# First loads, early spectrum, inverse tables and first norms of a two-layer conv and FFN kernel rearranged

## The chip, the cores and the metric

The kernel runs on one core of one Trainium2 chip. Its time is device microseconds per execution, the median over the runs. A profiled execution gives a span (first to last instruction) and a trace of every engine: PE (TensorE), DVE (VectorE), ACT (ScalarE), POOL (GpSimd) and SP (which only issues DMAs).

## The reference

Two layers, each a gated long convolution (A) and a SwiGLU block (B), on 2048 rows of 512 channels in bf16:

```python
def _A_ref(q, k, v, shift_k, ssm_k, ssm_D):
    # k_shift: a causal shift filter of 4 taps per channel
    for t in range(ks):
        k_shift = k_shift + k_pad[:, t:t + S, :] * shift_k[:, ks - 1 - t][None, None, :]
    kv = k_shift * v
    ...  # y = causal convolution of kv with ssm_k over 2048 rows, by FFTs of 4096
    y = y + kv * ssm_D[None, None, :]
    return q * y

def _B_ref(x, w_gate, w_up, w_down):
    return (_silu(x @ w_gate) * (x @ w_up)) @ w_down      # 512 -> 1792 -> 512

x = A_q
x = x + _A_ref(_layernorm(x), A_k, A_v, A_shift_k, A_ssm_k, A_ssm_D)
x = x + _B_ref(_layernorm(x), B_w_gate, B_w_up, B_w_down)
x = x + _A_ref(_layernorm(x), A_k, A_v, A_shift_k, A_ssm_k, A_ssm_D)
x = x + _B_ref(_layernorm(x), B_w_gate, B_w_up, B_w_down)
```

The convolution y does not depend on x, so it is computed once and serves both layers.

## The kernel before, in words

**Blocks.** The 2048 rows are cut into NB = 4 blocks of 512 rows. A block lies on the 128 partitions with R = 4 consecutive rows on each (row = 4p + r), 512 channels along the free dimension. The convolution is done block by block with transforms of length 1024 written as matmuls: `fwd` holds 14 tables of 128x128 (cosine and sine for each residue r, and their negatives), `inv` the same tables transposed. For each block the kernel makes the spectrum of its filter block h (`H`, `G`), the spectrum of its k-shifted times v rows (`X`), the products of spectra that meet in an output block (`Z`), and the inverse (`Y`).

**Start of the program, block 0.** What runs first needs the first loads and tables that are made on the chip.

- The loads: `load_k(0)` (L361) and `load_h(0)` (L356) and the row of ssm_D (`drow`) on ACT's DMA queue, in this order; the taps (`tapR`), `load_v(0)` and `load_x(0)` on SP's. The gate weights `wg` go to SP's queue too, but a one-element copy on POOL (L901) that reads h and writes `wg_sb` holds them until h has landed. Behind them on SP's queue: h and k of block 1, `wu`, `wd`.
- The tables: POOL makes index ramps, DVE the phases `ph` (8 blocks, L908, L913), ACT takes the Sin (two halves of `fwd`, L915), DVE the negated blocks (L921). `inv` comes from 14 PE transposes of `fwd` (L957) and two ACT copies (L959).
- The shift filter as matmuls: the taps are turned on PE (`turn_taps`), and for each 128 channels (`dt`) and each tap j a diagonal matrix `dg[dt, j]` is made from the identity: 3 groups on DVE (L937), the fourth on ACT (L934, four activations). k is turned with 16 PE transposes (`transpose_k`, L379) and copied to `kTb`. `shift_mul` (L487) is then 64 matmuls of 128 columns into four PSUM tiles, each multiplied into `vt` on DVE (L503).
- h is turned with 16 PE transposes (`transpose_h`, L476), copied to `hs`, and `drow` is added to its row 0 (L943). `half` (L430) makes half of h's spectrum with 8 matmuls of 512 columns; twice, with `butterfly` behind each on DVE. `direct` (L454) makes X in 32 matmuls, `product` Z on DVE (L621, L625), `inverse_direct` (L684) Y in 32 matmuls with `inv`.
- The layer norms of block 0's rows: `ln_stats` on DVE (bn_stats L707), the power of -0.5 on POOL (L712), `normalise` on DVE (L755). There is a form on ACT as well, `ln_stats_act` (L716), with accumulating activations.

**FFN units.** Each (layer, block, half block of 256 rows) is a unit `ffn` (L808): 112 matmuls of 256 columns for gate and up, Silu and copies on ACT, a product on DVE (L845), and 28 matmuls of 512 columns with `wd`, added to x by DVE (L871), or, for units in X_PE, by two more matmuls with the identity (L818). 16 units follow each other; the convolution work of the next blocks is put between their instructions.

**Order.** All instructions are first entered in a plan (`add`) with an engine, an assumed cost, an assumed latency for DMAs (`lat`), an optional due time, and PSUM or SBUF rings that they need. `forward` then plays the plan through and picks, engine by engine, the order of issue; the chip's engines run their instructions in this order. Constants steer it: DUR and T0 (due times of the units), STRETCH, HSL, ASL, SLK, and the sets ST1, ST2, Z_ACT, N_ACT, X_PE that say which engine does a norm or an addition. While the plan has PE idle before 32 us, `issue` fills the gap with matmuls of the identity (`wm`, L1024):

```python
n = int((start - t - 0.4) / 0.085)
```

Of the kernel before, what the change touches and what calls it, by code (L numbers as in the profile page):

```python
# [9 lines left out]
P = 128  # L10
# [9 lines left out]
SLK = 9.39  # L20
H_DMA = lambda b: b in {2, 3}
ST1 = lambda l, c, h: (l, c, h) in {(0, 2, 0), (0, 3, 1), (1, 0, 1)}
ST2 = lambda l, c, h: (l, c, h) in {(0, 1, 0), (0, 1, 1), (0, 3, 1), (1, 0, 0)}
ASL = 4.93
# [4 lines left out]
HSL = 8.56  # L29
Z_ACT = lambda l, c, h: (l, c, h) in {(0, 1, 1), (0, 3, 0), (0, 3, 1), (1, 0, 0), (1, 0, 1), (1, 1, 1), (1, 2, 0), (1, 2, 1), (1, 3, 1)}  # L30
N_ACT = lambda l, c, h: (l, c, h) in {(0, 2, 1), (0, 3, 0), (0, 3, 1), (1, 1, 0), (1, 3, 0)}
Z_DMA = lambda i, j: False
D_DMA = lambda l, c, h: False
X_PE = lambda l, c, h: (l, c, h) in {(0, 2, 0), (0, 2, 1), (1, 3, 1)}
RINGS = {}
T0, FLOOR = -4.91, -25.25
DUR = [25.78, 17.38, 27.0, 25.33, 24.61, 20.95, 21.66, 16.0, 20.19, 21.8, 21.11, 25.85, 19.67, 26.45, 17.91, 25.24]
STRETCH = {1: {"PE": 5.28, "DVE": 1.49, "ACT": 3.3, "POOL": 1.0, "SP": 110.68},
           2: {"PE": 1.3, "DVE": 1.9, "ACT": 1.37, "POOL": 1.0, "SP": 1.4},
           3: {"PE": 2.03, "DVE": 1.56, "ACT": 1.6, "POOL": 1.0, "SP": 1.97}}  # L40
R = 4
# [3 lines left out]
NS = 8  # L45
# [21 lines left out]
class Plan:  # L67
# [182 lines left out]
    def issue(self, seq, place, when, warm_until, warm):  # L250
        t, busy = 0.0, {}
        for o in seq:
            start, end = when[o]
            if o.eng == "PE":
                if start < warm_until and start - t > 0.5:
                    for ring, i in [(r, i) for r in ("pf", "pd", "pc") for i in range(self.rings[r])]:
                        if busy.get((ring, i), 0.0) <= t:
                            n = int((start - t - 0.4) / 0.085)
                            if n > 0:
                                warm(ring, i, n)  # L260
                            break
                t = end
# [9 lines left out]
def kernel(  # L272
# [70 lines left out]
    tapT, drow = whole("tapT", [P, KD, KS]), new("jk", "drow", [1, D])  # L343
# [12 lines left out]
    def load_h(b, eng="SP", due=None, after=()):  # L356
        hn[b] = new("s8" if b == 1 else "h", "hn", [P, KD, L], parts=1)
        q = nc.sync if eng == "SP" else nc.scalar
        return add(eng, 0.55, lambda: q.dma_start(out=hn[b].t[:], in_=h3[:, :, b * L:(b + 1) * L]), w=[hn[b]], lat=(5.5, 10.0)[b] if b < 2 else 6.0, due=due, after=after)

    def load_k(b, due=None, after=()):  # L361
        if b == 0:
            kn[b] = new("s8", "kn", [P, R, D])
            add("ACT", 0.5, lambda: nc.scalar.dma_start(out=kn[b].t[:], in_=k_t[:, b]), w=[kn[b]], lat=4.6, due=due)
            return
# [4 lines left out]
    def transpose_k(b, ring, engs):  # L370
# [3 lines left out]
        for dt in range(KD):  # L374
            pt = new(ring, "pt", [P, R, P], BF16)
# [13 lines left out]
    def load_v(b, due=None, after=()):  # L389
        vt[b] = new("v", "vt", [P, R, D], parts=R)  # L390
        return add("SP", 0.6, lambda: nc.sync.dma_start(out=vt[b].t[:], in_=v_t[:, b]), w=[vt[b]], lat=4.5 if b else 5.0, due=due, after=after)

    def load_x(c, due=None, after=()):
        xs[c] = new("x", "xc", [P, R, D], parts=R)
        return add("SP", 0.7, lambda: nc.sync.dma_start(out=xs[c].t[:], in_=q_t[:, c]), w=[xs[c]], lat=4.5 if c else 6.0, due=due, after=after)
# [34 lines left out]
    def half(rows, ev, par, scale, ring, engs, conv):  # L430
        for ch in ("ac", "bd")[par]:
            slot = "abcd".index(ch)
            for part in (0, 1):
# [3 lines left out]
                    r=[(rows, [r for _, r in terms]), fwd], w=[ps], conv=conv)  # L437
# [16 lines left out]
    def direct(rows, dst, ring, engs):  # L454
        for slot in (0, 2, 1, 3):
            c1, c2, sign = (("a", "c", 1), ("b", "d", 1), ("a", "c", -1), ("b", "d", -1))[slot]
            for part in (0, 1):
# [3 lines left out]
                add("PE", pe(4), lambda ps=ps, terms=terms: mm(ps.t[:], [(fT(f, r), rows.t[:, r, :]) for f, r in terms]),  # L461
                    r=[rows, fwd], w=[ps])
# [3 lines left out]
    def transpose_h(b, ring, order, conv, engs=("ACT",)):  # L466
        hs = new("hs", "hs", [P, R, D], parts=R)
        m = len(engs)
        for r0 in order:
# [9 lines left out]
            if engs[order.index(r0) % m] == "ACT":  # L479
                add("ACT", act(len(rows) * D), lambda pt=pt, sl=sl: nc.scalar.copy(out=hs.t[:, sl, :], in_=pt.t[:]),  # L480
                    r=[pt], w=[(hs, rows)], conv=conv)
            else:
# [4 lines left out]
    def shift_mul(b, ring, conv, after=()):  # L487
        for r in range(R):
# [7 lines left out]
            add("PE", pe(KS * KD, P), go, r=[kT[b], dg], w=[ps], conv=conv, after=after)  # L496
            if KV_ACT and b:
# [3 lines left out]
                    [ks], [(vt[b], (r,))], conv=conv)  # L501
                continue
            dve(D, lambda ps=ps, r=r: nc.vector.tensor_tensor(out=vt[b].t[:, r, :], in0=ps.t[:], in1=vt[b].t[:, r, :],  # L503
                                                             op=ALU.mult), [ps], [(vt[b], (r,))], one=True, conv=conv)
# [90 lines left out]
    def spectrum_x(b):  # L595
        if K_ACT(b):
            shift_mul_t(b)
        else:
            shift_mul(b, "pc", True, first if b == 1 else ())
# [84 lines left out]
    def inverse_direct(k, slots_order):  # L684

        y, z = new_y(k), Z[k]
        pss = [new(("pd", "pd", "pc", "pc")[r], "ps", [P, D], F32) for r in range(R)]
# [28 lines left out]
    def ln_stats_act(c, rows):  # L716
# [3 lines left out]
        for o, i in enumerate(rows):  # L720
            jk = new("jk", "jk", [P, D])
            add("ACT", 0.62, lambda jk=jk, o=o, i=i: nc.scalar.activation(
                out=jk.t[:], in_=xs[c].t[:, i, :], func=ACT.Copy, accum_out=sm.t[:, o:o + 1]), r=[(xs[c], (i,))], w=[jk, (sm, (o,))])
# [17 lines left out]
    def shift_of(st, n):  # L741
# [3 lines left out]
                                                                op0=ALU.mult, op1=ALU.mult), r=[mv, rstd], w=[nmr])  # L745
# [15 lines left out]
    def apply_norm(c, h, layer=0):  # L761
        rows = range(HP * h, HP * h + HP)
        st = ln_stats_act(c, rows) if ST1(layer, c, h) else ln_stats(c, rows)
        nmr = shift_of(st, HP) if N_ACT(layer, c, h) else None
# [5 lines left out]
    def prologue(layer, c, h, on_pe=False):  # L770
# [21 lines left out]
        st = ln_stats(c, rows)  # L792
        done = []
        for o, i in enumerate(rows):
# [7 lines left out]
            pop = add("PE", pe(KD, P), go, r=[z, ident], w=[pt])  # L802
            add("ACT", act(D), lambda pt=pt, o=o: nc.scalar.copy(out=zT.t[:, :, o, :], in_=pt.t[:]), r=[pt], w=[(zT, (o,))])
            done = [zop, pop]
        return done


    def ffn(unit):  # L808
# [81 lines left out]
    load_k(0, -70)  # L890
    tapR = new("dn", "tapR", [KD, P, KS])
    add("SP", 0.5, lambda: nc.sync.dma_start(out=tapR.t[:], in_=A_shift_k.rearrange("(dt p) j -> dt p j", p=P)), w=[tapR],
        lat=4.3, due=-70)
    load_h(0, "ACT", -59)
    ph = new("s8", "ph", [P, NS, P], I32, parts=2)
    load_v(0, -59)
    add("ACT", 0.5, lambda: nc.scalar.dma_start(out=drow.t[:], in_=A_ssm_D.rearrange("(o d) -> o d", o=1)), w=[drow], lat=5.0,
        due=-58)
    load_x(0, -58)

# [157 lines left out]
```

## Time and profile before

| | |
|---|---|
| median of 5 runs | 354.87 us (354.57 to 355.17) |
| profiled execution | 355.17 us, span 353.4 us |
| PE busy | 347.8 us (98%), 2716 matmuls |
| DVE busy | 276.5 us (78%) |
| ACT busy | 249.7 us (71%) |
| POOL busy | 38.5 us (11%), 42 instructions |
| HBM read, written | 12.33 MB, 2.10 MB |

Busy times of PE are modelled (matmuls are pipelined), so the spacing of starts tells more than the share. In the chain of waits each step is what released the next one; "issue" is time in which an engine waited for nothing that the profile shows. In a table by stage, each engine's busy time stands with its number of instructions in brackets.

### The profile page before, as it was taken

Reading aid. Unit: us, or ns where it says so; the run is one execution under the profiler, and the core shown is the slowest. Engines: PE = TensorE matmul, PEld = TensorE weight load, DVE = VectorE, ACT = ScalarE, POOL = GpSimd, SP = SyncE. Lnnn points to the kernel's source line nnn. Section 1 sums busy time; section 2 is a strip of 40 time slices with the busy share of each in tenths; the row PEclk is TensorE's granted clock in tenths of the full one; section 3 lists DMA queues with packets and bytes.
Section 4 is the critical chain, followed back from the end, with each engine's and each line's share of the span. In section 5 each row is a group of like instructions: output and inputs, shape, how many; then the busy total and the mean of one; then the engine's idle time right before and its main releaser. Section 6 shows DMA issues by size and latency. Waiting matters only on the chain.

```text
span 353.4 us, 6784 instructions
## 1 busy us (share of the span) xinstructions
PE 347.8 (98%) x2716; PEld 255.0 (72%) x2716; DVE 276.5 (78%) x511; ACT 249.7 (71%) x470; POOL 38.5 (11%) x42
## 2 busy tenths in 40 slices
PE   7999999999999999999999999999999999999996
PEld 7745976867778686858677676758687777778673
DVE  4997999999989999999997999799973323545111
ACT  4768684859897865758869994946488975646452
POOL 1001010111102110111220010201111000001000
PEclk9999999999999999999999999999999999999999
DMA  6999230010333222012101033010102010101100
GB/s 238 294 346 302 48 81 10 2 30 2 72 109 77 76 89 32 0 32 60 32 32 31 14 108 61 0 32 1 32 30 32 30 32 1 24 8 24 38 2 30
DMA packets 37898, 21.98 MB, mean 62 GB/s; under 512 B 29798, under 2 KB 35691, under 8 KB 37867
## 3 DMA queue, kind: packets, MB, share of 16 engines
q1 hardware_dynamic: 37192, 20.51, 22.2%
q10 hardware_dynamic: 674, 1.05, 0.9%
q8 instruction: 21, 0.34, 0.4%
q14 instruction: 11, 0.08, 0.1%
HBM read 12.33 MB, written 2.10 MB: 41 GB/s over the span
## 4 chain that ended last, share of the span: by engine, by line
PE 65%; DVE 26%; ACT 4%; issue 2%; POOL 2%; ACTq 0%; DVEq 0%; POOLq 0%
PE pf L335 36%; PE pd L852 18%; PE ps L335 8%; DVE ht L845 3%; DVE bnst L707 3%; DVE m L519 2%; DVE t L636 2%; DVE t L652 2%; DVE t L642 2%; ACT H L424 2%; DVE Z L657 2%; PE wm L1024 2%; DVE G L556 1%; DVE xc L778 1%; POOL rstd L712 1%
## 5 line engine op out<-in xcount | busy, mean ns | idle before, releaser
L335 PE MATMUL pf<-zT,wg_sb 128*128 128x256 bf16 x896 | 116.1, 273 | 0.2 <-ACT sg L838 0.2
L335 PE MATMUL pf<-zT,wu_sb 128*128 128x256 bf16 x896 | 116.1, 273 | 0.0
L852 PE MATMUL pd<-wd_sb,ht 128*128 128x512 bf16 x448 | 103.1, 379 | 0.0
L335 PEld LDWEIGHTS <-wg_sb 128*128 128x128 bf16 x896 | 87.6, 98 | 19.3 <-issue 0.7
L335 PEld LDWEIGHTS <-wu_sb 128*128 128x128 bf16 x896 | 87.6, 98 | 11.4
L838 ACT ACTIVATE sg<-pf 128x512 bf16<-128x512 f32 x112 | 67.6, 604 | 26.0 <-PE pf L335 25.8
L842 ACT CAST ht<-pf 128x512 bf16<-128x512 f32 x112 | 66.2, 591 | 18.6 <-PE pf L335 18.1
L852 PEld LDWEIGHTS <-ht 128*128 128x128 bf16 x448 | 43.8, 98 | 47.1
L845 DVE TENSOR_TENSOR ht<-ht,sg 128x1024 bf16<-128x1024 bf16 x64 | 39.4, 619 | 33.3 <-ACT ht L842 33.3
L712 POOL TENSOR_TENSOR rstd<-ve,nhalf 128x2 f32<-128x2 f32 x25 | 29.1, 1163 | 207.0 <-DVE ve L710 185.8
L707 DVE BATCH_NORM_STATS2 bnst<-xc 128x6 f32<-128x512 bf16 x50 | 32.3, 684 | 0.5
L864 ACT CAST dn<-pd 128x512 bf16<-128x512 f32 x26 | 14.0, 590 | 25.0 <-PE pd L852 25.0
L636 DVE TENSOR_TENSOR t<-X,G 128x2048 bf16<-128x2048 bf16 x18 | 21.9, 1218 | 0.0
L642 DVE TENSOR_TENSOR t<-X,G 128x2048 bf16<-128x2048 bf16 x18 | 21.9, 1218 | 0.0
L871 DVE TENSOR_TENSOR xc<-xc,dn 128x1024 bf16<-128x1024 bf16 x13 | 8.9, 688 | 15.9 <-ACT dn L864 15.8
L424 ACT ACTIVATE X<-ps 128x512 bf16<-128x512 f32 x32 | 18.6, 604 | 2.0 <-PE ps L335 1.9
L751 ACT ACTIVATE z<-xc,nmr,rstd 128x512 bf16<-128x512 bf16 x18 | 13.6, 807 | 2.8 <-DVE nmr L744 2.7
L737 POOL TENSOR_TENSOR rstd<-ve,nhalf 128x2 f32<-128x2 f32 x7 | 7.8, 1118 | 70.4 <-DVE ve L733 70.4
L335 PE MATMUL ps<-vt,fwd 128*128 128x512 bf16 x56 | 15.2, 379 | 0.0
L335 PEld LDWEIGHTS <-fwd 128*128 128x128 bf16 x96 | 9.3, 98 | 7.9 <-issue 0.2
L652 DVE TENSOR_TENSOR t<-t,t 128x2048 bf16<-128x2048 bf16 x12 | 14.7, 1222 | 0.1
L657 DVE TENSOR_TENSOR Z<-Z,t 128x2048 bf16<-128x2048 bf16 x12 | 14.7, 1221 | 0.1
(96 smaller groups left out, 318.0 us busy)
## 6 DMA issues: line engine op xcount, KB each, us to landing
vt<-in_A_v_dram SPq DMA_DIRECT2D x4, 512.0 KB, 4.0
xc<-in_A_q_dram SPq DMA_DIRECT2D x4, 512.0 KB, 4.8
out_dram<-xc SPq DMA_DIRECT2D x16, 128.0 KB, 1.8
wg_sb<-in_B_w_gate_dram SPq DMA_DIRECT2D x1, 1792.0 KB, 7.5
wu_sb<-in_B_w_up_dram SPq DMA_DIRECT2D x1, 1792.0 KB
wd_sb<-in_B_w_down_dram SPq DMA_DIRECT2D x1, 1792.0 KB, 13.5
hn<-in_A_ssm_k_dram SPq DMA_DIRECT2D x3, 512.0 KB, 6.1
kn<-in_A_k_dram ACTq DMA_DIRECT2D x1, 512.0 KB, 3.3
```

Source lines behind the costliest of these rows:

```text
L335: nc.tensor.matmul(o, lhsT=lhsT, rhs=rhs, start=(n == 0), stop=(n == len(terms) - 1))
L424: add("ACT", act(D), lambda: nc.scalar.activation(out=view(), in_=ps.t[:], func=ACT.Copy, scale=scale), r=[ps], w=[(buf, keys)], conv=conv)
L636: dve(n * D, lambda t1=t1, part=part: nc.vector.tensor_mul(out=t1.t[:], in0=x.t[:, sl, 0, :], in1=g.t[:, sl, part, :]), [(x, key(slots, (0 ...
L642: dve(n * D, lambda t2=t2, part=part: nc.vector.tensor_mul(out=t2.t[:], in0=x.t[:, sl, 1, :], in1=g.t[:, sl, 1 - part, :]), [(x, key(slots ...
L652: dve(n * D, lambda t1=t1, t2=t2, comb=comb: nc.vector.tensor_tensor(out=t1.t[:], in0=t1.t[:], in1=t2.t[:], op=comb), [t2], [t1], conv=conv)
L657: dve(n * D, lambda t1=t1, part=part: nc.vector.tensor_add(out=z.t[:, sl, part, :], in0=z.t[:, sl, part, :], in1=t1.t[:]), [t1], [zk], con ...
L707: add("DVE", 0.6, lambda st=st, i=i: nc.vector.bn_stats(out=st.t[:], in_=xs[c].t[:, i, :]), r=[(xs[c], (i,))], w=[st])
L712: add("POOL", PW, lambda: nc.gpsimd.tensor_tensor(out=rstd.t[:], in0=ve.t[:], in1=nhalf.t[:].to_broadcast((P, n)), op=ALU.pow), r=[ve, nha ...
L838: add("ACT", act(D), lambda ps=ps, o=o, sg=sg: nc.scalar.activation(out=sg.t[:, o:o + 2, :], in_=ps.t[:], func=ACT.Silu), r=[ps], w=[(sg, ...
L842: add("ACT", act(D), lambda ps=ps, o=o, ht=ht: nc.scalar.copy(out=ht.t[:, o:o + 2, :], in_=ps.t[:]), r=[ps], w=[(ht, (o // 2,))], due=(uni ...
L845: dve(n * W, lambda sg=sg, ht=ht: nc.vector.tensor_mul(out=ht.t[:], in0=ht.t[:], in1=sg.t[:]), [sg], [ht], due=(unit, k / pairs, 0.0, "h"))
L852: nc.tensor.matmul(pds[o].t[:], lhsT=ht.t[:, q, o * P:(o + 1) * P], rhs=wt["d"].t[:, ft, :], start=(ft == 0 and not xpe), stop=(ft == NF - 1))
```

## The change

- h of block 0 is the first and, but for `drow`, the only load on ACT's queue; k goes to SP's queue, behind the taps and ahead of v and x. The copy on POOL that held `wg` is gone; `wg` follows x on SP's queue.
- `inv` comes from two DMA transposes of `fwd` on SP's queue, behind `wg` and ahead of h and k of block 1, `wu` and `wd`; the 14 PE transposes and two ACT copies go.
- h is turned first, its row 0 is copied together with the addition of `drow` (now 128 rows of zeros but for the first), and half "ac" of its spectrum is entered ahead of the taps and of k. The other half, "bd", comes behind the shift and the first slot of `direct`. The `direct` matmuls are entered in groups of two terms.
- The diagonals of two `dt` go to POOL (8 instructions), two stay on DVE; the two negations of table blocks go to POOL.
- The norms of block 0 in layer 0, both halves, are taken on ACT, the second half after the first half's z.
- The filler's count, several assumed latencies and due times, PSUM rings, the constants and the engine sets are new.

```diff
-SLK = 9.39
+SLK = 8.59
-ST1 = lambda l, c, h: (l, c, h) in {(0, 2, 0), (0, 3, 1), (1, 0, 1)}
-ST2 = lambda l, c, h: (l, c, h) in {(0, 1, 0), (0, 1, 1), (0, 3, 1), (1, 0, 0)}
-ASL = 4.93
+ST1 = lambda l, c, h: (l, c, h) in {(0, 2, 0), (0, 3, 0), (1, 0, 1)}
+ST2 = lambda l, c, h: (l, c, h) in {(0, 1, 0), (0, 1, 1), (1, 0, 0)}
+ASL = 2.32
-HSL = 8.56
-Z_ACT = lambda l, c, h: (l, c, h) in {(0, 1, 1), (0, 3, 0), (0, 3, 1), (1, 0, 0), (1, 0, 1), (1, 1, 1), (1, 2, 0), (1, 2, 1), (1, 3, 1)}
-N_ACT = lambda l, c, h: (l, c, h) in {(0, 2, 1), (0, 3, 0), (0, 3, 1), (1, 1, 0), (1, 3, 0)}
+HSL = 18.8
+Z_ACT = lambda l, c, h: (l, c, h) in {(0, 1, 1), (0, 3, 0), (0, 3, 1), (1, 0, 0), (1, 0, 1), (1, 1, 1), (1, 2, 0), (1, 2, 1)}
+N_ACT = lambda l, c, h: (l, c, h) in {(0, 3, 0), (0, 3, 1), (1, 1, 0), (1, 3, 0), (1, 3, 1)}
-X_PE = lambda l, c, h: (l, c, h) in {(0, 2, 0), (0, 2, 1), (1, 3, 1)}
+X_PE = lambda l, c, h: (l, c, h) in {(0, 1, 0), (0, 1, 1), (0, 2, 1), (1, 3, 1)}
...
-                            n = int((start - t - 0.4) / 0.085)
+                            n = int((start - max(t, 1.0) - 0.3) / 0.106)
...
-        return add(eng, 0.55, ..., w=[hn[b]], lat=(5.5, 10.0)[b] if b < 2 else 6.0, due=due, after=after)
+        return add(eng, 0.55, ..., w=[hn[b]], lat=(4.1, 10.0)[b] if b < 2 else 6.0, due=due, after=after)
...
-            add("ACT", 0.5, lambda: nc.scalar.dma_start(out=kn[b].t[:], in_=k_t[:, b]), w=[kn[b]], lat=4.6, due=due)
+            add("SP", 0.5, lambda: nc.sync.dma_start(out=kn[b].t[:], in_=k_t[:, b]), w=[kn[b]], lat=4.2, due=due)
...
-            pt = new(ring, "pt", [P, R, P], BF16)
+            pt = new("pc" if dt < 2 else "pd", "pt", [P, R, P], BF16)
...
-        pss = [new(("pd", "pd", "pc", "pc")[r], "ps", [P, D], F32) for r in range(R)]
+        pss = [new(("pd", "pd", "pf", "pf")[r], "ps", [P, D], F32) for r in range(R)]
...
-    load_k(0, -70)
+    load_h(0, "ACT", -70)
     tapR = new("dn", "tapR", [KD, P, KS])
...
-        lat=4.3, due=-70)
-    load_h(0, "ACT", -59)
+        lat=3.4, due=-70)
+    load_k(0, -69)
...
     load_v(0, -59)
+    add("POOL", 0.3, lambda: nc.gpsimd.memset(drow.t[:], 0.0), w=[drow], due=-60)
...
-    load_x(0, -58)
-    add("POOL", 0.1, lambda: nc.gpsimd.tensor_copy(out=wt["g"].t[0:1, 0, 0:1], in_=hn[0].t[0:1, 0, 0:1]), r=[hn[0]], w=[wt["g"]])
-    wg = load_weights("g", -57)
+    x0 = load_x(0, -58)
...
-        add("DVE", 0.28, lambda src=src, dst=dst: nc.vector.tensor_scalar(
+        add("POOL", 0.6, lambda src=src, dst=dst: nc.gpsimd.tensor_scalar(
             out=fwd.t[:, dst, :], in0=fwd.t[:, src, :], scalar1=-1.0, scalar2=None, op0=ALU.mult),
             r=[(fwd, (n,))], w=[(fwd, (part,))])
+    wg = load_weights("g", -57, after=[x0])
+    for n in range(2):
+        sl = slice(n * NI, (n + 1) * NI)
+        tabs = add("SP", 2.2, lambda sl=sl: nc.sync.dma_start_transpose(
+            out=inv.t[:, sl, :], in_=fwd.t[:, sl, :].rearrange("p k f -> p (k f)")), r=[fwd], w=[(inv, (n,))], lat=8.0, due=-56.8,
+            after=[wg])
+    load_h(1, "SP", -56.5, after=[tabs])
+    load_k(1, -56.4, after=[tabs])
+    load_weights("u", -56, after=[tabs])
+    load_weights("d", -55, after=[tabs])
+    hs = transpose_h(0, "pf", (0, 2, 1, 3), False, ("DVE", "ACT"), drow)
+    ev = spectrum("ev")
+    G[0] = H[0] = spectrum("G0")
+    half(hs, ev, "ac", 2.0 / N, "pf", ("ACT", "DVE"), False, -60)
...
-    for j in range(KS):
-        add("ACT", 0.32, lambda j=j: nc.scalar.activation(out=dg.t[:, KD - 1, j, :], in_=ident.t[:], func=ACT.Copy,
-                                                          scale=tapF.t[:, KD - 1, j:j + 1]), r=[ident, tapF], w=[(dg, (KD - 1,))])
-    for dt in range(KD - 1):
+    for dt in (KD - 2, KD - 1):
+        for j in range(KS):
+            add("POOL", 0.35, lambda dt=dt, j=j: nc.gpsimd.tensor_scalar(out=dg.t[:, dt, j, :], in0=ident.t[:],
+                                                                         scalar1=tapF.t[:, dt, j:j + 1], scalar2=None, op0=ALU.mult),
+                r=[ident, tapF], w=[(dg, (dt,))])
+    for dt in range(KD - 2):
...
+    transpose_k(0, "pc", ("ACT", "DVE"))
+    shifted = shift_mul(0, "pf", False, due=-49)
+    normed[0, 0, 0] = apply_norm(0, 0, on_act=True, due=-47)
+    butterfly(ev, G[0], 0, False)
     X[0] = spectrum("X0")
-    direct(vt[0], X[0], "pf", ("ACT", "ACT"))
+    direct(vt[0], X[0], "pf", ("ACT", "ACT"), (0,))
+    half(hs, ev, "bd", 2.0 / N, "pf", ("ACT", "ACT"), False)
+    butterfly(ev, G[0], 1, False)
+    direct(vt[0], X[0], "pf", ("ACT", "ACT"), (2, 1, 3))
...
-    first = prologue(0, 0, 0, True)
+    first, stats = prologue(0, 0, 0, True)
+    normed[0, 0, 1] = apply_norm(0, 1, on_act=True, after=first)
     prologue(0, 0, 1)
```

DUR, STRETCH, T0 (-4.91 to -8.68) and FLOOR are new as well.

## The prediction

> **What bounds the kernel now.** I read the page's 40 slices first, then the PE timeline, the chain of waits, the windows, and the DMA issues of the first 9 us. PE is busy in every slice:
>
> ```profile
> PE   7999999999999999999999999999999999999996
> PEclk9999999999999999999999999999999999999999
> ```
>
> The PE timeline shows what it does (start, us, instructions):
>
> ```profile
> 1.73 5.35 PE L1024 MATMUL wm<-ident 128*128 128x128 bf16 x51 [1.73 <-POOL ident masks.py:199]
> 7.33 1.07 PE L379 MATMUL pt<-ident,kn 128*128 128x128 bf16 x16
> ...
> 9.24 1.11 PE L476 MATMUL pt<-ident,hn 128*128 128x128 bf16 x12
> ...
> 10.53 3.73 PE L335 MATMUL ps<-dg,kTb 128*128 128x128 bf16 x64
> 14.10 3.73 PE L335 MATMUL ps<-hs,fwd 128*128 128x512 bf16 x16
> ...
> 35.89 1.03 PE L335 MATMUL pf<-zT,wg_sb 128*128 128x256 bf16 x8
> ```
>
> From 10.53 the matmuls start back to back. Spacings in the timeline are 0.109 us (256 columns), 0.216 (512) and 0.058 (128). From 35.89 to 350.0 there are 1792 of 256, 518 of 512 and 112 shift matmuls of 128 columns: 195.6 + 111.9 + 6.5 = 314.0 us in a stretch of 314.1. From 10.53 to 35.89 the same count gives 25.0 of 25.4. So retuned constants (DUR, HSL, the sets) have no idle PE time to recover after 10.53; they can only lose some. What can be gained lies ahead of 10.53, and there the chain of waits reads:
>
> ```profile
> 1.73 5.37 PE wm L1024 x51
> ...
> 7.79 0.46 issue
> 8.24 0.98 ACT dg L934 x3
> 9.23 0.47 ACT kTb L384
> 9.70 0.30 ACT dg L934
> 10.00 0.48 ACT hs L480
> ...
> 10.53 14.20 PE ps L335 x112
> ```
>
> PE runs 51 filler matmuls (wm) until 7.08; its queue is in order, so the k transposes wait for them. But k had landed long before:
>
> ```profile
> vt<-in_A_v_dram SPq DMA_DIRECT2D x1, 512.0 KB, 4.2
> xc<-in_A_q_dram SPq DMA_DIRECT2D x1, 512.0 KB, 6.4
> ...
> kn<-in_A_k_dram ACTq DMA_DIRECT2D x1, 512.0 KB, 3.3
> hn<-in_A_ssm_k_dram ACTq DMA_DIRECT2D x1, 512.0 KB, 6.8
> ```
>
> With the issue starts added (0.73, 1.16, 1.17, 1.59) k lands at 4.0, v at 5.4, h at 8.0, x at 8.0. The filler's end, some 3 us after k, is what starts the kernel, and h at 8.0 is next.
>
> **The start, step by step.** I compare the moment T at which the 64 shift matmuls start: 10.53 now, and from there PE is full. In the changed kernel the first half of the h spectrum (8 matmuls x 0.216 = 1.73) is done before T, so the end moves by 10.53 + 1.73 - T = 12.26 - T.
>
> *Filler.* The count is int((4.8 - 0.4)/0.085) = 51 now (tapR planned at 0.5 + 4.3). With 3.4 for tapR, and max(t, 1.0) in it, it becomes int((3.9 - 1.0 - 0.3)/0.106) = 24; with a few more before h, PE is released at about 4.5 to 5.0.
>
> *h.* It was second on ACT's queue and landed at 8.0; first there, k would have been its row: 4.0. It now shares the engines with tapR and k on SP's queue. The windows show 53 GB/s in 1 to 2 us, 315 in 2 to 3, some 400 after; equal shares of 1.05 MB end near 4.7. Its 1 KB rows against k's 4 KB make it later rather than earlier. I take 4.9, between ends 4.1 and 8.0. k then takes v's place (5.4), v about 6.6, x stays near 8.0, as the total bytes are the same.
>
> *PE before T.* 4 tap transposes (0.25), 16 of h, 16 of k, 8 matmuls of 512. At full rate: 0.25 + 0.91 + 0.91 + 1.73 = 3.8. But the filler runs at 5.35/51 = 0.105 us each, and the k transposes after 7.33 at 0.057: the PE is at half rate until about 7, though the PEclk row shows 9 throughout. What is done before 7 therefore costs double. From 4.9, 16 of h end at 6.6 and 3 of k by 6.9; 13 x 0.057 more end at 7.6, the spectrum half at 9.4, with the taps 9.6. The hs copies (0.6 each, two engines, from 5.5) are ready by 7.2, under the k transposes.
>
> The Trainium skill, "TensorE: Matmul & The Clock Gate", Part 1, says the clock opens after about 3.4 us of sustained activity, in a free-running window. That speaks against starting real work early; with a start at 1.73 it would put the opening anywhere in 5.1 to 8.5, and T between 8.8 and 10.4 by an estimate from that page.
>
> *GpSimd.* It gets the two negations (128x384), the drow memset and 8 tap diagonals. No such row exists in the trace; the nearest are
>
> ```profile
> 1.38 0.29 POOL masks.py:199 TENSOR_SCALAR_AFFINE_SELECT ident<-ident 128x128 bf16<-128x128 bf16 x1
> 15.90 0.70 POOL L712 TENSOR_TENSOR rstd<-ve,nhalf 128x2 f32<-128x2 f32 x1 [7.37 <-DVE ve L710]
> ```
>
> and the groups' mean of 1.163 us for rstd beside a busy DVE. The first has the right shape: I take 0.35 to 0.5. Negations from 4.3 (the first Sin ends there) to 5.7, then 8 x 0.35 to 0.5 ends at 8.5 to 9.7: just under PE's 9.6. "SBUF — State Buffer", Who interferes with whom, has DVE and GpSimd exclude each other on a shared port where DVE reads two SBUF inputs. By that page only the two DVE diagonals (0.64 each) and the row-0 add's like would block, an estimated 1.3 us more, T near 10.5.
>
> *DVE before T.* Two hs (0.66 + 0.64), taps 0.2, two dg 1.28, two kTb 1.28: 4.1 us from 5.5 is 9.6 at the latest. Three engines meet at 9.6, so T = 9.7 and the gain is 2.56 us.
>
> **The rest.** The 14 table transposes leave PE, but they stood in the hole before 10.53; PE gains nothing, ACT 1.74 us that it was not short of. X_PE grows from three to four units: 2 x 0.216 = 0.43 us more on PE in the full stretch. Sum: 2.56 - 0.43 = 2.13.
>
> The inverse tables go to SP's queue. SP waits there for the negations (to 5.7) and behind it are h1, k1, wu, wd, v1. wg now starts right after x: 2.1 + 1.84 MB at 400 GB/s ends near 12. The tables need 2.5 us (zT's landing) to 10.5 us (kTb's) after that: 14.5 to 22.5. First use is 24.57 now, 22.4 then; the cover is the direct products, and if it were gone each us late is a us of PE, less 1.2 us of hn transposes. k1 is issued near 12 to 17 (9.54 now), lands 10.5 later at 27.5 at worst, used at 32.8. wu is issued at 20 to 26 and lands, like now, some 9.5 later (30 to 35.5), used near 37; wd lands by 40, used near 44.5. All cost nothing, with 2 us left at the least.
>
> First norms on ScalarE: four rows leave DVE: bn_stats, aggregates and ve 3.0, normalise 1.46; negations 0.52, the drow add 0.40 and one dg 0.64 go too; two ev copies (1.2) and about 1.0 of small ops come. DVE is lighter by 3.8 us before 35. This matters, because in the middle the chain runs through DVE:
>
> ```profile
> 100.00:150.00 50.00, 50.00 (x412) 38.71 (x410) 48.33 (x77) 37.91 (x76) 6.47 (x4) 1.00 0.24 61
> 150.00:207.00 57.00, 57.00 (x420) 40.90 (x418) 53.74 (x97) 46.02 (x86) 8.80 (x7) 1.00 0.17 43
> ```
>
> (third busy figure: DVE, 95%). PE 2.1 us ahead needs DVE 2.1 us ahead: 3.8, and 0.7 of constants before 207 (two xc adds of 0.69 out, one normalise pair in). That covers it. The new PSUM rings and due values, the split of the direct products and the dropped wg gate change order alone; their cover is that PE always has another ready matmul, and their price if not is in the tail below. ACT gets two rows of Copy 0.63, Square 0.73, two accumulator reads of 0.2 and normalise 0.80, 5.1 us for each half of the block; the first half falls where ACT idles (12.6 to 14.7) and replaces the tables' 1.74 and the dg's 1.3; the second, after the first z, stands behind h1's spectrum at 30 to 34 and delays only the second unit, 20 us off.
>
> **The rivals.** (A) As worked out: 355.17 - 2.13 = 353.0 against the profiled execution (span 353.4 + 1.77 outside), which lies 0.30 above the median; on the median 352.7.
> (B) The clock opens early, h lands near 4.1: start 4.6 plus 3.8, T = 8.4, gain 3.43: 351.4. For it: k's row. Against: half rate until 7.
> (C) h on its own queue does not land earlier: its small rows lose to k, v and x, and it lands at 8.0 as now. PE's order has it first, so T = 8.0 + 0.9 + 0.9 + 1.73 = 11.5, gain 0.33: 354.5. For: total bytes are unchanged. Against: k landed at 4.0 while v shared.
> (D) GpSimd as slow as rstd's mean: negations end at 6.7, 8 x 1.163 = 9.3, T = 16.0; the shift, in PE's order and by the ring's order ahead of the other half, stalls PE: 12.26 - 16.0 - 0.43 = -4.2: 359.0. It makes the kernel slower once a diagonal takes over 0.85 us (T past 12.5). For: two-column rstd at 0.7 to 1.16. Against: 0.29 for the right shape.
>
> **How the numbers follow.** A 0.62, B 0.13, C 0.14, D 0.11. I predict 352.7. A measurement of this kernel tells about 0.2% (0.7 us) from no change, so faster means under 354.16 and slower over 355.58. A and B are faster, but A's unknown costs (a late table, a DVE bind at 207) reach into no change: 0.04 of A; a quarter of C is faster. Faster 0.75, same 0.13, slower 0.12 (D and 0.01 of A's tail). For 8 in 10 the range takes A, most of B and most of C: 351.0 to 355.0.
>
> **What would show it.** Right: some 24 to 31 wm instead of 51; hn transposes at about 5 spaced 0.105; dg on POOL at 0.35 to 0.5 each; the shift's first matmul at 9.7 and 64 matmuls unbroken after it; first wg_sb matmul near 33.8; no PE wait on inv; PE gapless to its end near 347.9. Wrong: hn landing after 6.5; dg on POOL over 0.85; a PE wait of over 1 us anywhere after 12; DVE still idle-free yet PE waiting on ACT or DVE near 207.

## The result, and the profile after

The changed kernel takes 355.88 us (355.02 to 357.34, 28 runs) against 354.79 (354.16 to 355.49, 51 runs) for the kernel before on the same chip: a ratio of 1.0033, 95% interval 1.0025 to 1.0040. It is slower by 1.1 us; 352.7 was forecast, and the time lies above the range. The profiled execution took 357.22 us with a span of 355.4; it lies 1.3 us above the median, so the waits below are those of a run on the long side.

The PE timeline of the changed kernel (start, us, instructions, and in brackets the idle time ahead and its releaser):

```profile
2.18 2.74 PE L1031 MATMUL wm<-ident 128*128 128x128 bf16 x24 [2.18 <-POOL ident masks.py:199]
...
5.07 1.08 PE L480 MATMUL pt<-ident,hn 128*128 128x128 bf16 x16
5.99 1.06 PE L379 MATMUL pt<-ident,kn 128*128 128x128 bf16 x16
7.62 1.89 PE L335 MATMUL ps<-hs,fwd 128*128 128x512 bf16 x8 [0.58 <-DVE hs L487]
9.35 1.17 PE L1031 MATMUL wm<-ident 128*128 128x128 bf16 x18
10.61 1.17 PE L335 MATMUL ps<-dg,kTb 128*128 128x128 bf16 x15
11.98 2.90 PE L335 MATMUL ps<-dg,kTb 128*128 128x128 bf16 x49 [0.20 <-POOL dg L952]
15.22 0.38 PE L463 MATMUL ps<-vt,fwd 128*128 128x512 bf16 x1 [0.34 <-DVE vt L510]
16.42 0.81 PE L463 MATMUL ps<-vt,fwd 128*128 128x512 bf16 x3 [0.82 <-DVE vt L510]
...
25.40 1.46 PE L703 MATMUL ps<-Z,inv 128*128 128x512 bf16 x6
```

The early part goes as forecast: 24 filler matmuls instead of 51, h turned from 5.07, half of its spectrum done by 9.4. Then PE stands twice. The shift's 64 matmuls end near 14.7 where the forecast had 13.3, and behind them three holes wait for the products with v. The inverse starts at 25.40; it was 24.57 before, and 22.4 in the forecast.

The shift's wait is GpSimd's. Its timeline, the negations and the tap diagonals that the change gave it:

```profile
4.46 2.80 POOL L924 TENSOR_SCALAR fwd<-fwd 128x384 bf16<-128x384 bf16 x2 [2.17 <-ACT fwd L918]
7.25 4.67 POOL L952 TENSOR_SCALAR dg<-ident,tapF 128x128 bf16<-128x128 bf16 x8
```

A negation takes 1.40 us and a tap diagonal 0.58; the last one ends at 11.92, and PE's longer run starts at 11.98.

The holes behind the shift come from v. The chain of waits has them as one transfer, issued right behind x (L395) and the gate weights (L402):

```profile
1.59 0.41 SPq L395
...
2.04 0.43 SPq L402
...
2.52 11.86 DMA vt<-in_A_v_dram
```

The DMA issues of the first 9 us give the landing times (us from issue):

```profile
wg_sb<-in_B_w_gate_dram SPq DMA_DIRECT2D x1, 1792.0 KB, 11.1
hn<-in_A_ssm_k_dram ACTq DMA_DIRECT2D x1, 512.0 KB, 3.8
kn<-in_A_k_dram SPq DMA_DIRECT2D x1, 512.0 KB, 4.6
xc<-in_A_q_dram SPq DMA_DIRECT2D x1, 512.0 KB, 6.3
vt<-in_A_v_dram SPq DMA_DIRECT2D x1, 512.0 KB, 11.9
```

h, issued near 0.7, landed at 4.5 and k at 5.8. But v, which landed at 5.4 before, landed at 14.4, behind 1792 KB of wg. The diff leaves `load_v(0, -59)` as it was. What changed is its neighbours: the tables' transposes and h1 are now entered `after` wg, and wg `after` x, so the plan gives x and wg earlier due times than v's −59 and issues them first. Before, the one-element copy on GpSimd held wg until h had landed; it was issued at 8.56, now at 2.04.

All of PE's waits on other engines, longest first (us in total, times, longest):

```profile
PE wm L1031 <- POOL ident masks.py:199: 2.2, 1, 2.2
PE ps L463 <- DVE vt L510: 1.6, 3, 0.8
PE ps L335 <- DVE hs L487: 0.6, 1, 0.6
PE pf L335 <- ACT sg L847: 0.5, 1, 0.5
PE pd L861 <- DVE ht L854: 0.2, 1, 0.2
PE ps L335 <- POOL dg L952: 0.2, 1, 0.2
```

After the shift PE waits 2.3 us: 1.6 for v's products and 0.7 in the middle. The same list of the kernel before has 0.2 after its shift.

### The profile page after: what moved, and what is told of

Same layout as the page of the kernel before. It is cut to its first block, busy times and chain, and to the rows that moved or that the text cites. A ratio compares the mean times of both kernels' runs of the same rounds, so it can differ in the third digit from the quotient of the medians.

```text
span 355.4 us, 6752 instructions
## 1 busy us (share of the span) xinstructions
PE 346.6 (98%) x2694; PEld 252.4 (71%) x2694; DVE 274.5 (77%) x505; ACT 248.2 (70%) x472; POOL 50.9 (14%) x52
## 4 chain that ended last, share of the span: by engine, by line
PE 55%; DVE 32%; DMA 3%; POOL 3%; ACT 3%; issue 2%; SPq 0%; ACTq 0%; DVEq 0%; POOLq 0%
PE pf L335 31%; PE pd L861 16%; PE ps L335 4%; DVE ht L854 4%; DMA vt<-in_A_v_dram 3%; DVE bnst L715 3%; DVE m L527 3%; DVE t L650 3%; DVE t L660 2%; DVE t L644 2%; PE ps L703 2%; DVE Z L665 2%; PE ps L463 2%; POOL rstd L720 2%; POOL rstd L745 1%
## 5 line engine op out<-in xcount | busy, mean ns | idle before, releaser
L861 PE MATMUL pd<-wd_sb,ht 128*128 128x512 bf16 x448 | 100.8, 379 | 0.3 <-DVE ht L854 0.2
L847 ACT ACTIVATE sg<-pf 128x512 bf16<-128x512 f32 x112 | 68.6, 613 | 15.8 <-PE pf L335 14.6
L720 POOL TENSOR_TENSOR rstd<-ve,nhalf 128x2 f32<-128x2 f32 x24 | 28.9, 1204 | 197.5 <-DVE ve L718 182.1
L873 ACT CAST dn<-pd 128x512 bf16<-128x512 f32 x24 | 12.9, 589 | 29.6 <-PE pd L861 29.6
L715 DVE BATCH_NORM_STATS2 bnst<-xc 128x6 f32<-128x512 bf16 x48 | 31.0, 684 | 0.4
L745 POOL TENSOR_TENSOR rstd<-ve,nhalf 128x2 f32<-128x2 f32 x8 | 12.9, 1613 | 75.0 <-DVE ve L741 75.0
L867 ACT CAST xc<-pd 128x512 bf16<-128x512 f32 x8 | 4.3, 589 | 17.7 <-PE pd L861 17.7
L759 ACT ACTIVATE z<-xc,nmr,rstd 128x512 bf16<-128x512 bf16 x16 | 12.2, 807 | 4.8 <-DVE nmr L752 4.7
L737 ACT ACTIVATE jk<-xc,nm 128x512 bf16<-128x512 bf16 x16 | 11.9, 744 | 4.8 <-DVE nm L733 4.8
L660 DVE TENSOR_TENSOR t<-t,t 128x2048 bf16<-128x2048 bf16 x12 | 14.7, 1223 | 0.2
L785 DVE TENSOR_TENSOR n<-n,Yk 128x1024 bf16<-128x1024 bf16 x15 | 10.4, 692 | 5.6 <-ACT n L759 4.0
## 6 DMA issues: line engine op xcount, KB each, us to landing
wg_sb<-in_B_w_gate_dram SPq DMA_DIRECT2D x1, 1792.0 KB, 11.1
```

The costliest lines, as they stand in the source:

```text
L660: dve(n * D, lambda t1=t1, t2=t2, comb=comb: nc.vector.tensor_tensor(out=t1.t[:], in0=t1.t[:], in1=t2.t[:], op=comb), [t2], [t1], conv=conv)
L715: add("DVE", 0.6, lambda st=st, i=i: nc.vector.bn_stats(out=st.t[:], in_=xs[c].t[:, i, :]), r=[(xs[c], (i,))], w=[st])
L720: add("POOL", PW, lambda: nc.gpsimd.tensor_tensor(out=rstd.t[:], in0=ve.t[:], in1=nhalf.t[:].to_broadcast((P, n)), op=ALU.pow), r=[ve, nha ...
L745: add("POOL", PW, lambda: nc.gpsimd.tensor_tensor(out=rstd.t[:], in0=ve.t[:], in1=nhalf.t[:].to_broadcast((P, n)), op=ALU.pow), r=[ve, nha ...
L847: add("ACT", act(D), lambda ps=ps, o=o, sg=sg: nc.scalar.activation(out=sg.t[:, o:o + 2, :], in_=ps.t[:], func=ACT.Silu), r=[ps], w=[(sg, ...
L861: nc.tensor.matmul(pds[o].t[:], lhsT=ht.t[:, q, o * P:(o + 1) * P], rhs=wt["d"].t[:, ft, :], start=(ft == 0 and not xpe), stop=(ft == NF - 1))
```

## The experiments

Three theories stood after this; the recorded expectations call the part of the third that lies in the constants S. **W**: v behind wg on SP's queue makes the time. **P**: GpSimd's negations and diagonals, slower than forecast, make it. **M**: the newly set constants and order of the middle give back any earlier start (the middle is what lies behind the inverse, the first units above all). "Before" is the kernel before, run beside each on the same chip.

| kernel | median us | ratio to before, 95% interval |
|---|---|---|
| after | 355.88 | 1.0033 (1.0025 to 1.0040) |
| v_first | 354.72 | 0.9997 (0.9988 to 1.0005) |
| v_first_again (another chip) | 355.14 | 1.0006 (0.9996 to 1.0016) |
| neg_dve | 356.03 | 1.0035 (1.0024 to 1.0047) |
| v_first_neg_dve | 354.63 | 0.9992 (0.9982 to 1.0001) |
| no_pool_dg | 354.98 | 1.0007 (0.9998 to 1.0015) |
| bd_first | 356.30 | 1.0036 (1.0024 to 1.0049) |
| v_first_norm_dve | 354.64 | 0.9999 (0.9988 to 1.0011) |
| v_first_xpe3 | 359.22 | 1.0116 (1.0095 to 1.0136) |
| old_constants | 358.34 | 1.0095 (1.0076 to 1.0115) |
| before_v_late | 356.64 | 1.0052 (1.0039 to 1.0065) |
| before_filler | 354.08 | 0.9978 (0.9970 to 0.9987) |
| filler_h_first | 353.85 | 0.9975 (0.9964 to 0.9986) |

**v_first**: v issued ahead of x and wg, in the changed kernel.

```diff
-    load_v(0, -59)
+    load_v(0, -62)
```

> The changed kernel, with block 0's v issued ahead of x and of the gate weights on SP's queue (its due time -62 instead of -59; nothing else moves but two DVE positions and 14 fillers). Theory W (the loss is v's place: it lands at 14.4 us, behind 1.8 MB of wg): v lands near 6.6, the first product into vt starts by 12.3 instead of 14.47, the PE holes of 0.38 + 0.98 + 0.57 us between the shift and the direct products close, and the time falls by 1.9 us or a little more: about 354.0, ratio to the kernel before 0.998. Theory P (the loss is GpSimd: two negations of 1.4 us and eight diagonals of 0.58 hold the shift to 11.98): v ends its wait but the shift still ends at 14.8 and the time stays at 355.9. Theory S (the loss is the retuned constants: 0.5 us of PE idle in 100 to 150 and 0.5 in 150 to 207): no change, 355.9.

Its PE timeline, from the shift to the inverse:

```profile
11.95 2.90 PE L335 MATMUL ps<-dg,kTb 128*128 128x128 bf16 x49 [0.20 <-POOL dg L952]
14.68 0.81 PE L463 MATMUL ps<-vt,fwd 128*128 128x512 bf16 x3
...
23.32 1.03 PE L703 MATMUL ps<-Z,inv 128*128 128x512 bf16 x4
```

v lands at 7.3, nothing waits for it, and the inverse starts 2.08 us earlier than in the changed kernel. Timed, 0.0036 of 354.9 comes back, 1.3 us of the 1.9 expected; by the second pair of runs (v_first_again) 0.0027, 1.0 us. Within the intervals that is the whole loss against before, and W is shown. It is not the gain that was forecast: the kernel is now level with before.

**neg_dve**: the two negations back on DVE, v still late.

```diff
-        add("POOL", 0.6, lambda src=src, dst=dst: nc.gpsimd.tensor_scalar(
+        add("DVE", 0.28, lambda src=src, dst=dst: nc.vector.tensor_scalar(
...
```

> The changed kernel with the two negations of table blocks back on DVE (L924), v still behind wg. The diagonals on GpSimd then start near 5.4 instead of 7.25 and, at 0.58 each, end near 10.1 instead of 11.92. Theory P: the shift starts at 10.1 and the time falls by about 1.8 us to 354.1. Theory W: v still lands at 14.4, the shift ends early and waits, and the time stays within 0.3 of 355.9. Theory S: 355.9.

The 64 shift matmuls now run unbroken from 10.03, but then wait for v: `vt` 2.6 us instead of 1.6, and the time is the changed kernel's. The negations were hidden behind v's landing.

**v_first_neg_dve**: both edits.

> Both edits together. If v's place hides GpSimd's delay (W first, P behind it), the two gains add: the shift starts near 10.1, no hole after it, about 352.2, ratio 0.993. If W alone matters 354.0, if P alone 354.1, by S alone 355.9.

The shift's longer run starts at 10.95 and the inverse at 22.32, exactly 1.0 us earlier than in v_first. The time does not follow: the two ratios are 0.0005 apart, within their intervals. At unit 0's first gate matmul 0.66 us of the lead is left (35.40 for 36.06), and it is gone where unit 2 starts. Timeline of v_first_neg_dve, the norm of unit 2, its turning by DMA, and the first gate matmul:

```profile
69.46 2.20 POOL L745 TENSOR_TENSOR rstd<-ve,nhalf 128x2 f32<-128x2 f32 x1 [7.92 <-DVE ve L741]
...
72.73 3.21 SPq L792 DMA_TRANSPOSE zT<-z  x2
...
77.19 1.03 PE L335 MATMUL pf<-zT,wg_sb 128*128 128x256 bf16 x8 [0.69 <-DMA zT<-z]
```

The same norm and matmul in v_first's timeline, the matmul with no wait:

```profile
69.88 1.06 POOL L745 TENSOR_TENSOR rstd<-ve,nhalf 128x2 f32<-128x2 f32 x1 [7.92 <-DVE ve L741]
...
77.09 1.03 PE L335 MATMUL pf<-zT,wg_sb 128*128 128x256 bf16 x8
```

With a start a whole microsecond apart, unit 2 begins within 0.1 us of the same moment. Its z depends on DVE's aggregates and GpSimd's power. Of PE's 1.0 us the aggregates kept 0.42 (the power starts at 69.46 for 69.88), and the power took 2.20 us where it took 1.06 in v_first, so it ended 0.7 us later. Where DVE lost the rest stands below, in the part on the prediction.

**no_pool_dg**: v first, negations on DVE, and the diagonals as before (three groups on DVE, one on ACT): all of GpSimd's new work undone but the filling of `drow` with zeros.

> The changed kernel with v early, the negations on DVE and the tap diagonals as in the kernel before (three groups on DVE, one on ACT): nothing of the start on GpSimd but the memset and the ramps. Theory P: diagonals are ready near 8.5 instead of 10.9, the shift starts near 9.3 and the time falls another 0.8 us under v_first_neg_dve: 353.8. Theory M (behind v's place the next limit is the middle: unit 2 waits for its zT, 77.1 us, behind a DVE queue without a gap): the start gets earlier by 0.5 to 1, the end of unit 3 stays at 120, and the time stays at 354.6.

The shift runs unbroken from 9.99. PE then waits 0.7 us for ACT's zT at 36.33, 0.74 for the DMA's zT at 78.16 and 0.39 for ACT at 149.65, and the time is again that of before. So GpSimd set the changed kernel's shift, but freeing it buys nothing while the middle gives the lead back.

**bd_first**: the changed kernel with the "bd" half of h's spectrum entered ahead of the first direct product, as a cover for late v.

```diff
-    direct(vt[0], X[0], "pf", ("ACT", "ACT"), (0,))
-    half(hs, ev, "bd", 2.0 / N, "pf", ("ACT", "ACT"), False)
+    half(hs, ev, "bd", 2.0 / N, "pf", ("ACT", "ACT"), False, -48.5)
     butterfly(ev, G[0], 1, False)
+    direct(vt[0], X[0], "pf", ("ACT", "ACT"), (0,))
```

> The changed kernel, v still behind wg, but with the second half of the h spectrum (8 matmuls, 1.73 us) entered ahead of the first direct slot. Theory W with cover: it runs from the shift's end at 14.84 to 16.57, while v lands at 14.4 and the rows are multiplied; the holes of 1.93 us shrink to 0.5 or less and the time falls to 354.7, as with v early. Plain W: v is as late as before and the time stays at 355.9.

No gain. The PE timeline shows why:

```profile
15.70 0.59 PE L335 MATMUL ps<-hs,fwd 128*128 128x512 bf16 x2 [0.85 <-DVE vt L510]
```

The cover itself waits for `vt`: the four PSUM tiles of the shift are freed only by the products with v, and the spectrum's tiles come from the same ring. Work that needs no v could not start until v had landed.

**old_constants**: the changed start with all constants and sets of before.

> The changed kernel with all constants and engine sets of the kernel before (SLK, HSL, ASL, ST1, ST2, Z_ACT, N_ACT, X_PE, T0, FLOOR, DUR, STRETCH). Theory S: the idle us of PE between 100 and 207 goes, and two matmuls of X_PE (0.43) go: 354.5. Theories W and P: the start stays, v lands at 14.4 and the shift begins at 10.6 to 12; at most the 0.43 is gained: 355.4. A rise above 356 would say that the new constants were needed for the new start.

By the ratios 2.2 us more than the changed kernel; PE waits 2.8 us for zT. So the old constants do not suit the new start. Whether others than the new ones would suit it better was not tried.

**v_first_norm_dve**: v first, and block 0's two first norms back on DVE.

> The changed kernel with v ahead of x and wg (v_first), and block 0's two first norms as before: bn_stats on DVE, no accumulating activations on ACT, no dependence of the second on the first z. If the ACT norms take part in what is given back in the middle (unit 2's zT is late on ACT and SP): 0.5 to 1 us faster than v_first. If the forecast's view holds that they only relieve DVE, which is short in the middle: slower than v_first by up to 2 us, and DVE's first rows of Z and the first products come later. If they lie beside other work either way: the same within 0.3 us.

354.64 against v_first_again's 355.14 on the same chip, with overlapping intervals; PE's 0.7 us wait for unit 2's zT is there as well. The ACT norms neither make the middle's wait nor relieve it by an amount that this measurement can tell; it was not tried with the negations off GpSimd.

**v_first_xpe3** (with v_first_again beside it): v first, and the set of units that add x on PE as before, three instead of four.

```diff
-X_PE = lambda l, c, h: (l, c, h) in {(0, 1, 0), (0, 1, 1), (0, 2, 1), (1, 3, 1)}
+X_PE = lambda l, c, h: (l, c, h) in {(0, 2, 0), (0, 2, 1), (1, 3, 1)}
```

> The changed kernel with v ahead of x and wg on SP's queue (v_first), and the set X_PE of before: three units instead of four add to x on PE, so unit (0,1,0) and (0,1,1) add on DVE, (0,2,0) on PE. The forecast's term (PE has no idle time, so the two matmuls of 512 columns more cost 0.43 us): 0.4 us faster than v_first. The rival (DVE paces the stretch from 97 to 240, and each unit that adds on DVE gives it 2 x 0.69 us more there): no faster than v_first, 0.3 to 1.4 us slower.

> v_first once more, beside the two kernels that vary it, on the same chip. Expected 354.7 again, ratio to before 0.9997 within 0.001, v landing near 6.9, the shift's long run near 12 behind GpSimd's diagonals, the inverse near 23.3.

Both expectations for the set missed: 4.1 us slower than v_first_again. Unit 8 still starts as in v_first (198.61 for 198.53; 199.28 in v_first_again); then two pauses follow within 3 us. Windows of 5 us (busy time of PE, PEld, DVE, ACT and POOL with counts, then the granted clock):

```profile
200.00:205.00 5.00, 2.86 (x23) 2.08 (x22) 4.35 (x7) 5.00 (x9) 1.67 (x1) 1.00 0.00 0
205.00:210.00 5.00, 4.76 (x29) 3.63 (x29) 4.93 (x9) 5.00 (x10) 1.66 (x1) 0.66 0.16 54
```

ACT is full: six `ka` activations of block 3's shift (4.06 us from 198.86) stand ahead of the evacuation that PE needs, and two more ahead of the Silu. PE waits 0.95 and 1.43 us, and the granted clock of the 5 us that follow is 0.66 in the mean. As the plan reorders the instructions after such an edit, the 0.43 us that the forecast charged for the fourth unit can't be read from this run; it stays untested.

**before_v_late**: the kernel before without the gate on wg, with x and wg ahead of v.

> The kernel before, with SP's queue in the changed kernel's order: the gate of wg by POOL is gone, and v follows x and wg; all compute instructions keep their order. v then lands near 13 to 14 us instead of 5.4. Theory W, plain (a late v costs what it costs in the changed kernel): 1.2 us slower, 356.1. Theory W with cover (what makes v's lateness cost is that the half of the h spectrum that stood between the shift and the direct products has gone ahead of the shift, and the other half is held behind the first direct slot by the order of the pf ring): here 16 spectrum matmuls, 3.5 us, stand between the shift's end at 14.1 and the first direct matmul, so PE has no hole over 0.5 us and the time stays within 0.7 us of 354.9; DVE loses 2.2 us in its queue, which could show later.

It is 1.8 us slower, but not through v. Its PE timeline:

```profile
9.96 0.41 PE L476 MATMUL pt<-ident,hn 128*128 128x128 bf16 x4 [2.21 <-DMA hn<-in_A_ssm_k_dram]
...
11.33 5.36 PE L335 MATMUL ps<-dg,kTb 128*128 128x128 bf16 x64
```

Without the gate h, on the other queue, took 8.8 us instead of 6.8. PE paused 2.2 us for it, and the 64 matmuls after that took 5.36 us instead of 3.73. v landed at 13.0 (issued at 2.06, 10.9 us), when the late shift had only just begun, so nothing waited for it; the cover that before's order has for v, 16 spectrum matmuls behind the shift, was not put to the test. So the order of the loads was a cost in both kernels, by different tensors.

**before_filler**: the kernel before with nothing but the shorter filler (33 matmuls).

```diff
-                            n = int((start - t - 0.4) / 0.085)
+                            n = int((start - max(t, 1.0) - 0.3) / 0.106)
```

> The kernel before with the changed kernel's count of fillers alone: 33 instead of 51 ahead of the taps; the order of all other instructions is the same. The prediction's reading (the fillers' end at 7.08 starts the kernel): the k transposes start near 5.3, the shift starts at 9.2 to 9.5, after h has landed at 8.0, and the time falls by 1.0 to 1.3 us to 353.7. Rival, the clock: PE then idles from 6.5 to 8.0, is still at half rate when h is turned, and the shift's 64 matmuls run at 0.107: no gain, up to 3 us of loss. Rival, ACT's chain (dg, kTb, hs) sets the shift: no change, 354.9.

Faster than both kernels by this one line. Its PE timeline:

```profile
8.17 0.41 PE L476 MATMUL pt<-ident,hn 128*128 128x128 bf16 x4 [0.57 <-DMA hn<-in_A_ssm_k_dram]
...
9.59 3.74 PE L335 MATMUL ps<-dg,kTb 128*128 128x128 bf16 x64
...
23.52 0.81 PE L695 MATMUL ps<-Z,inv 128*128 128x512 bf16 x3
```

The shift starts 0.94 us earlier than in before, and every one of the 16 units ends 1.0 to 1.1 us earlier, to the last (349.0 for 350.1). In before's order an earlier start is carried to the end. Timed, the medians are 0.8 us apart, but the lowest times of the two only 0.3 (353.98 and 354.29 on this chip) and the highest 1.1 (354.35 and 355.44). The long filler was not always as long: in before_v_late the same 51 matmuls took 4.32 us, because their spacing went from 0.107 to 0.056 at 4.5 us after the span's start instead of 6.6. That this is why before's runs lie so far apart was not tested.

**filler_h_first**: before_filler with block 0's h first on ACT's queue and k behind the taps on SP's, the gate on wg kept.

> The kernel before with the shorter filler count (as in before_filler, 354.08 us, where PE waited for h until 8.17), and with one more part of the change: block 0's h first on ACT's queue, k behind the taps on SP's. Constants, tables, norms and diagonals as in before; wg still waits for h. The plan reorders some work by itself (half of the inverse tables' transposes move ahead of the taps'). The forecast's reading (a start that comes earlier is carried to the end): h lands near 4.6, k near 5.8, v near 6.5, the 64 shift matmuls start near 8.8 instead of 9.59, time 353.3. The rival (a start earlier than the one that the constants were set for is given back in the middle): the shift starts as early, and the time is 354.1 or more.

h lands at 4.6 and nothing waits for it, but the shift did not start earlier: the plan put 14 table transposes and k's ahead of h's, at half rate, and it starts at 9.95. 353.85 us is the lowest median of all, 0.9975 of before; before_filler's 0.9978 is not distinguishable from it. The expected start of 8.8 was missed, and as it was not earlier than before_filler's, this run does not decide on M.

## Why the prediction was wrong, by its own steps

The forecast's sum can be checked on every kernel, since T, the shift's start, can be read from each profile as the shift's end less the 3.57 us that it lasted before. The third column is 353.4 − (12.26 − T − 0.43), for before's order 353.4 − (10.53 − T); the fourth PE's waits after the shift's end; the fifth adds them, less the 0.2 us that before has.

| kernel | T | span by the sum | waits | with waits | span measured |
|---|---|---|---|---|---|
| forecast | 9.7 | 351.3 | none | 351.3 | |
| after | 11.14 | 352.7 | 2.3 | 354.8 | 355.4 |
| neg_dve | 10.03 | 351.6 | 3.0 | 354.4 | 355.1 |
| v_first | 11.11 | 352.7 | 0.4 | 352.9 | 352.7 |
| v_first_again | 11.12 | 352.7 | 0.7 | 353.2 | 353.5 |
| v_first_neg_dve | 10.11 | 351.7 | 1.5 | 353.0 | 352.9 |
| no_pool_dg | 9.99 | 351.6 | 1.8 | 353.2 | 353.8 |
| before_filler | 9.59 | 352.5 | 0.0 | 352.3 | 352.3 |
| filler_h_first | 9.95 | 352.8 | 0.2 | 352.8 | 352.8 |

Each row is one execution, and those of the kernel before alone have spans from 352.3 to 353.7, so an agreement closer than that is partly luck. The rule "PE is full from T, so the end follows T" holds in before's order to 0.2 us without the waits. In the changed order it misses by up to 3.5 us (neg_dve), and with the waits added by 0.7. Part of that rest is how a wait is counted: from the modelled end of a matmul, 0.38 us for 512 columns, while the next could have started after 0.216, so each pause costs some 0.16 us more than its entry. Of the 4.1 us between the forecast's span and the changed kernel's profiled one, 1.44 is T, 2.1 is v (with the same T the inverse starts at 25.40, in v_first at 23.32), and 0.6 is lost behind the inverse.

- **What bounds the kernel: right.** before_filler shows that the filler's end set the start, and that h, near 8.0, was next: PE waited for it until 8.17.
- **h: right.** 4.9 was taken, 4.5 measured. Its 1 KB rows did not make it late: it took 3.8 us from issue, k's 4 KB rows 4.6. Rival C is out. Rival B's conditions, an early h and an early clock, were nearly met in the changed kernel's profile, and brought nothing, as GpSimd and v came after.
- **"k then takes v's place (5.4), v about 6.6": wrong, and the step that made the change slower.** k landed at 5.8, v at 14.4. The forecast saw that wg starts right after x, but it worked out wg's effect on the tables and on h1 alone, and took SP's order for the order of the lines. It asked of every queue what a moved step costs and not who is overtaken when a gate goes. Undone, it is worth 1.0 to 1.3 us. Its signs of being wrong watched h, the diagonals, single waits of over 1 us after 12, and PE near 207; none of them came (v's three waits were at most 0.82 each).
- **GpSimd: the mechanism was named, the size was off.** Negations 1.40 each against 0.7, diagonals 0.58 (0.67 in neg_dve) against 0.35 to 0.5. The row taken, an affine select of 0.29, was the nearest by shape but no neighbour in operation. Rival D's threshold of 0.85 per diagonal took the negations at 0.7 for granted; with 1.4 a diagonal of 0.58 was enough to hold T at 11.1. What GpSimd's company would cost DVE, put at 1.3 us by an estimate, came to 0.3 on the two diagonal groups (1.60 us, and 1.29 in no_pool_dg). In the changed kernel v's landing hid it (neg_dve), and with v first the time did not follow either (v_first_neg_dve).
- **"That covers it": wrong, and the step that kept the gain away.** DVE was to be 3.8 us lighter and so to keep up with an earlier PE. Two kernels that start the shift 1.0 and 1.1 us earlier than v_first (v_first_neg_dve and no_pool_dg) get 1.1 and 1.4 us more of waits. With v and GpSimd's work both put back, no_pool_dg is still 2.3 us above the forecast. The profiles show where the lead goes. In v_first_neg_dve DVE runs 1.00 us ahead of v_first until 32.0, and then stands at the first product of block 1 with its v:

```profile
33.27 0.76 DVE L507 TENSOR_TENSOR vt<-ks,vt 128x512 bf16<-128x512 bf16 x2 [1.26 <-PE ps L335]
```

  In v_first there is no wait:

```profile
33.16 0.92 DVE L507 TENSOR_TENSOR vt<-ks,vt 128x512 bf16<-128x512 bf16 x2
```

  The profile names PE as the releaser, but PE's matmuls and ACT's copies for the two products had ended by 32.6. What came at that moment is block 1's v: issued on SP's queue at 22.51, behind `wu` and `wd` (17.47 and 18.10), it took 10.6 us and landed at 33.1. In no_pool_dg it landed at 34.1 and DVE waited 1.64 us; in v_first, though issued 1.0 us later, at 31.9, before it was needed. ACT's next copy waits for the product and stands ahead of zT's copies, and PE then waits 0.40 us (0.70 in no_pool_dg) for zT at unit 0. So v of block 1 sat behind weights as v of block 0 had, and did not come earlier with PE. The forecast has this load in SP's queue and gives it no landing time; it counted DVE's work, not when the pieces come up. In before's order there is room: in before_filler this v lands at 33.5, and DVE takes these products only at 40.58. At unit 2 DVE is 0.42 us ahead again, and there GpSimd's power takes 1.1 us longer. All this is read from traces: no run moves this load alone, and why the power took twice as long is open. v_first_norm_dve gives no sign that the ACT norms are the cause.
- **Tables by DMA: right for `inv`.** They landed at 15.3 and 17.7 and no kernel's PE waited for `inv`.
- **The clock: not a constant.** The forecast had half rate until 7. In the changed kernel's profile the h transposes ran at full rate from 5.07 (16 in 1.08 us), 2.9 us after the first filler matmul. In v_first and neg_dve, with the fillers at the same times, they took 1.90 and were at half rate, in v_first_again 1.33. In v_first the spacing went from 0.107 to 0.056 only at 8.1, 5.9 us after the first filler. It did not show in the time: with the negations on GpSimd T was 11.14, 11.11 and 11.12.

The Trainium skill, "TensorE: Matmul & The Clock Gate", Part 1, lets the clock open after about 3.4 us of activity in a free-running window and warns that the moment varies from run to run. The variation agrees with these runs; the page's figure lies between the 2.9 us of the changed kernel and the 5.9 of v_first.

## What to carry to other kernels

When a change takes away a gate or adds an order between transfers, write down the new order of every queue it touches and which early tensor is now behind the big one: here a line that the diff did not touch, the load of v, moved behind 1.8 MB and cost the whole difference. An earlier start is worth its length only if the inputs further on move with it, so look for the first ones that another engine or a queue brings (here the v of block 1, then a norm, turned by DMA) and check when they are ready, not how busy that engine is. And try the cheapest edit alone first: one line, the filler count, gave more than the whole rearrangement.

## What the runs showed of the hardware that was not expected

- In three profiles PE ran at half rate after pauses of about 2 us. After 2.21 us of waiting (before_v_late) 64 matmuls of 128 columns took 5.36 us instead of 3.73; after 0.95 and 1.43 us close together (v_first_xpe3) the granted clock of the next 5 us was 0.66; after 2.17 us (old_constants, at 83.25) 8 gate matmuls took 1.87 us instead of 1.03. Pause and slow matmuls together cost about 1.7 times the pause in the first two. Not every pair of pauses does it: after 1.39 and 0.82 us (neg_dve) the granted clock stayed at 1.00. The table of advice in "TensorE: Matmul & The Clock Gate" ("Why this matters for your kernels") speaks of gaps over about 3 us; these were shorter.
- A load can be slowed by one on the other queue: with wg let go on SP's queue, h on ACT's queue took 8.8 us instead of 6.8.
- On GpSimd a multiplication by a scalar takes 1.40 us for 128x384 and 0.58 to 0.67 for 128x128 in bf16; DVE needs 0.26 for the first. Beside GpSimd's negations a DVE diagonal group took 0.80 us (1.60 for two); with GpSimd free of both jobs 0.65 (1.29 for two).
- One program can differ in the middle alone: the two profiles of the changed kernel with v first have the same start (inverse at 23.32 in both) and spans of 352.7 and 353.5. Unit 3 starts 0.08 us apart in them (97.97 and 98.05), unit 4 0.46, unit 6 0.75, and the last 0.76.
